# A cosine gate without Abs on ScalarE, and four pieces of work moved beside it

## The chip, the cores and the metric

The kernel runs on one core of one Trainium2 chip. The metric is the device time of one execution in microseconds (us), and a stated time is the median of several executions. PE is TensorE (matmuls), PEld its weight loads, ACT ScalarE, DVE VectorE, POOL GpSimd. "L467" is line 467 of the kernel whose profile is shown; the same line of the program has slightly other numbers in other kernels.

## The reference

Cross attention between tokens and 32 state rows per head makes a matrix of 4352 rows and 512 columns, which goes through a two-layer network whose gate is h times cos(h):

```python
scores = scale * x @ state.T          # softmax, then a @ state        (x reads)
scores2 = scale * state @ x.T         # softmax, then a2 @ x           (state reads)
x = concatenate([xread, sread])       # -> (4352, 512)
h = x @ w_in                          # (4352, 2048)
g = h * np.cos(h)
return g @ w_out                      # (4352, 512)
```

The two weight matrices arrive as 64-bit floats; ACT, DVE and POOL convert them on the way, in five pieces per block.

## The kernel before

The work is cut into 144 tiles ("steps"): per batch of 512 tokens 16 hidden tiles of 128 x 512, and 16 smaller ones for the states. One step, in the order of the program (cuts marked; the conversions run only in the first steps):

```python
def hidden(t):                        # PE: 2 matmuls into one of two PSUM buffers
    t.hp = hps.tile([P, S], F32, name="h")[:, 0:t.n]
    ...
def gate(t):                          # ACT: h + 1.5 * 2**23, to round h to an integer
    nc.scalar.activation(t.q, t.hp, func=ACTF.Copy, bias=MAGIC)
def gate2(t):                         # DVE: (q - MAGIC) - h
    nc.vector.scalar_tensor_tensor(out=t.q, in0=t.q, scalar=MAGIC, in1=t.hp,
                                   op0=ALU.subtract, op1=ALU.subtract)
def gate3(t):                         # ACT: |q|, then sin(pi/2 - 2 pi |q|) = cos(2 pi h)
    nc.scalar.activation(t.q, t.q, func=ACTF.Abs)
    nc.scalar.activation(t.q, t.q, func=ACTF.Sin, bias=halfpi, scale=-TWO_PI)
def gate4(t):                         # DVE: the product h * cos, into a slot of g_all
    nc.vector.tensor_tensor(t.g, t.hp, t.q, op=ALU.mult)
...
for step, t in enumerate(all_tiles):
    hidden(t)
    go(0)                             # attention work of PE
    gate(t); gate2(t)
    if step == 3:
        part(0, "products", 1, SIDE)
        part(0, "products_kept", 1, SIDE)      # two evictions on ACT
    go(1); go(3)                      # attention work of ACT, of DVE
    convert(last, "bcdf")             # DVE: shift, xor; POOL: sum; next load
    convert(conv, "1")                # ACT: first half of a conversion
    gate3(t); gate4(t)
    convert(conv, "2")                # ACT: second half
    go(2); go(4)                      # more attention work of ACT (exponentials), DVE
    ...                               # POOL: block sums; PE: outputs of earlier steps
```

(h is held divided by 2 pi.) After each batch's scores, ACT takes exponentials, which need another activation table than Sin: at these changes the trace has 15 table loads, 1.28 us each.

## Time and profile before

787.93 us, median of 3 executions (786.89 to 788.06); the profiled execution took 786.81 us with a span of 785.0 us at a granted clock of 1.00.

| engine | busy us | share of the span |
|---|---|---|
| PE | 765.1 | 97% |
| DVE | 417.3 | 53% |
| ACT | 389.1 | 50% |
| POOL | 176.7 | 23% |

The table alone says that PE is nearly full. What it can't say is which of PE's 20 idle microseconds wait for what: that is in the timeline, whose lines end with the idle time before a group and who ended it. The prediction shows those lines.

### The profile page before, as it was taken

How to read it: one execution, taken by the hardware profiler on the slowest of the kernel's cores; microseconds unless marked ns; L12 is line 12 of the kernel's file. 1: busy time of each engine (PE TensorE's matmuls, PEld its weight loads, DVE VectorE, ACT ScalarE, POOL GpSimd, SP SyncE). 2: the span in 40 equal slices, each digit the busy share in tenths (PEclk: the TensorE clock that was granted, in tenths of full speed). 3: DMA queues.
4: the chain of work that ended last, by engine and by line, in shares of the span. 5: the costliest groups of instructions: out<-in, count | busy, mean ns of one | idle time of the engine just before them, and what ended most of it. 6: DMA issues, size and time to landing. Idle time of an engine off the chain costs nothing.

```text
span 785.0 us, 7535 instructions
## 1 busy us (share of the span) xinstructions
PE 765.1 (97%) x2664; PEld 340.3 (43%) x2664; DVE 417.3 (53%) x656; ACT 389.1 (50%) x626; POOL 176.7 (23%) x118
## 2 busy tenths in 40 slices
PE   8998899899999999999999999999999999999997
PEld 3443433344344444444344434434444444455554
DVE  5768778623563466734554467635554446431431
ACT  3888954733463545633473446443563445322222
POOL 2344359673000000641000001640000004610200
PEclk9999999999999999999999999999999999999999
DMA  8595451060011510250104310330100114000021
GB/s 241 167 263 187 141 100 28 4 104 1 3 25 31 102 24 5 34 101 0 24 5 76 58 27 15 54 67 0 28 1 0 28 28 130 4 0 15 13 41 40
DMA packets 161957, 43.49 MB, mean 55 GB/s; under 512 B 153920, under 2 KB 153920, under 8 KB 161920
## 3 DMA queue, kind: packets, MB, share of 16 engines
q1 hardware_dynamic: 161024, 42.49, 24.8%
q10 hardware_dynamic: 768, 0.39, 0.2%
q8 instruction: 21, 0.34, 0.2%
q0 software_dynamic: 128, 0.13, 0.1%
q14 instruction: 16, 0.13, 0.1%
HBM read 34.08 MB, written 8.91 MB: 55 GB/s over the span
## 4 chain that ended last, share of the span: by engine, by line
PE 81%; ACT 10%; DVE 6%; issue 1%; DMA 1%; SPq 0%; POOL 0%; DVEq 0%
PE o L532 44%; PE h L467 26%; PE at L314 4%; PE o L652 4%; PE at L404 2%; ACT q L482 1%; ACT q L481 1%; ACT s L228 1%; DVE q L476 1%; ACT q L473 1%; DVE g_all L488 1%; ACT xT L360 1%; ACT w_in L225 1%; ACT L482 1%; DVE xT L334 1%
## 5 line engine op out<-in xcount | busy, mean ns | idle before, releaser
L467 PE MATMUL h<-aT,sw 128*128 128x512 f32 x512 | 241.5, 594 | 11.0 <-DVE g_all L488 8.1
L532 PE MATMUL o<-g_all,w_out 128*128 128x512 f32 x512 | 236.4, 598 | 1.2 <-POOL w_out L239 1.2
L494 POOL TENSOR_TENSOR g_all<-g_all 128x512 f32<-128x512 f32 x80 | 112.1, 1423 | 451.5 <-DVE g_all L488 447.9
L473 ACT ACTIVATE q<-h 128x512 f32<-128x512 f32 (+1 forms) x144 | 82.1, 570 | 262.3 <-PE h L467 262.2
L476 DVE SCALAR_TENSOR_TENSOR q<-q,h 128x512 f32<-128x512 f32 (+1 forms) x144 | 94.2, 654 | 216.9 <-ACT q L473 216.9
L532 PE MATMUL o<-g_all,s 128*128 128x512 f32 x384 | 177.3, 598 | 0.0
L488 DVE TENSOR_TENSOR g_all<-h,q 128x512 f32<-128x512 f32 (+1 forms) x144 | 94.8, 658 | 124.8 <-ACT q L482 118.6
L467 PEld LDWEIGHTS h<-aT,sw 128*128 128x128 f32 x512 | 96.4, 190 | 135.4 <-issue 110.7
L532 PEld LDWEIGHTS o<-g_all,w_out 128*128 128x128 f32 x512 | 94.0, 190 | 125.5 <-issue 118.4
L481 ACT ACTIVATE q<-q 128x512 f32<-128x512 f32 (+1 forms) x144 | 87.6, 608 | 93.5 <-DVE q L476 93.4
L532 PEld LDWEIGHTS o<-g_all,s 128*128 128x128 f32 x384 | 70.8, 190 | 91.7 <-issue 87.3
L482 ACT ACTIVATE q<-q,halfpi 128x512 f32<-128x512 f32 (+1 forms) x144 | 100.5, 698 | 4.5
L239 POOL TENSOR_TENSOR w_out<-w_out,s 128x1024 int32<-128x1024 int32 x10 | 23.9, 2390 | 77.1 <-DVE w_out L234 73.5
L494 DVE TENSOR_TENSOR g_all<-g_all 128x512 f32<-128x512 f32 x48 | 33.2, 692 | 1.6
L441 ACT COPY sw<-at 128x512 f32<-128x512 f32 x50 | 26.8, 589 | 9.0 <-PE at L314 9.0
L467 PE MATMUL h<-sT,w_in 128*128 128x256 f32 x128 | 30.2, 379 | 0.0
L652 PE MATMUL o<-w_out,g_all 128*128 128x512 f32 x64 | 29.6, 592 | 0.0
L467 PEld LDWEIGHTS h<-sT,w_in 128*128 128x128 f32 x128 | 24.3, 190 | 10.1 <-issue 6.7
L239 POOL TENSOR_TENSOR w_in<-w_in,s 128x1024 int32<-128x1024 int32 (+1 forms) x10 | 19.3, 1929 | 38.8 <-DVE w_in L234 36.5
L314 PE MATMUL at<-w_in,stT 64*32 64x512 f32 x400 | 27.2, 601 | 0.0
L538 DVE SCALAR_TENSOR_TENSOR held<-o,held 128x512 f32<-128x512 f32 x40 | 25.3, 675 | 2.9 <-PE o L532 2.9
L559 DVE STREAM_TRANSPOSE ot<-held 128x512 f32<-128x512 f32 x32 | 22.1, 692 | 0.0
(80 smaller groups left out, 427.7 us busy)
## 6 DMA issues: line engine op xcount, KB each, us to landing
out_dram<-ot SPq DMA_DIRECT2D x132, 64.0 KB, 2.0
g_all<-in_moe_w_out_dram SPq DMA_DIRECT2D x8, 1024.0 KB, 4.9
g_all<-in_moe_w_in_dram SPq DMA_DIRECT2D x6, 1024.0 KB, 5.2
xT<-in_x_dram SPq DMA_DIRECT2D x96, 64.0 KB, 2.3
x_b<-in_x_dram SPq DMA_DIRECT2D x24, 256.0 KB, 4.6
x_b<-in_x_dram SPq DMA_DIRECT2D x16, 128.0 KB, 4.0
g_all<-in_moe_w_in_dram SPq DMA_DIRECT2D x4, 512.0 KB, 6.0
x_b<-in_moe_w_out_dram SPq DMA_DIRECT2D x1, 1024.0 KB, 5.9
```

The costliest lines, as they stand in the source:

```text
L239: nc.gpsimd.tensor_tensor(bits, bits, e, op=ALU.add)
L314: nc.tensor.matmul(out=(to or at)[j][Ns * k:Ns * k + Ns, 0:n], lhsT=w[D * j:D * j + D, self.b, Ns * k:Ns * k + Ns], rhs=r(slice(D * j, D * ...
L441: (copy or nc.scalar.copy)(sw_of[self.b, nt][:, j, c0:c1], to[j][:, 0:c1 - c0])
L467: nc.tensor.matmul(out=t.hp, lhsT=t.lhs(i), rhs=t.rhs(i), start=(i == 0), stop=(i == t.kn - 1))
L473: nc.scalar.activation(t.q, t.hp, func=ACTF.Copy, bias=MAGIC)
L476: nc.vector.scalar_tensor_tensor(out=t.q, in0=t.q, scalar=MAGIC, in1=t.hp, op0=ALU.subtract, op1=ALU.subtract)
L481: nc.scalar.activation(t.q, t.q, func=ACTF.Abs)
L482: nc.scalar.activation(t.q, t.q, func=ACTF.Sin, bias=halfpi, scale=-TWO_PI)
L488: nc.vector.tensor_tensor(t.g, t.hp, t.q, op=ALU.mult)
L494: engine.tensor_tensor(out, a, b, op=ALU.subtract)
L532: nc.tensor.matmul(out=acc[bank][ch], lhsT=w[:, i, P * ch:P * ch + P], rhs=g.g, start=(i == 0), stop=(i == NH - 1))
L652: nc.tensor.matmul(out=acc[MAIN][i], lhsT=t.g[:, P * i:P * i + P], rhs=w_out[:, :, t.f, :], start=(t.n_th == 0), stop=(t.n_th == NF - 1))
```

## The change

The intent is to take work off ACT. The gate converts h + 1/4 to an integer n (ACT's output is an integer). Rounded to nearest, n − h lies between −1/4 and 3/4 and pi/2 − 2 pi (n − h) between −pi and pi; Sin is given that directly, without Abs. The rounding was not looked at by itself. Around it four pieces of work move: five weight conversions, two evictions (copies of results out of PSUM, the matmuls' output memory), batch 1's last product copies, and the block sums (sums and differences of blocks of w_out on POOL, which later products use as weights). Cut to its core:

```diff
-        nc.scalar.activation(t.q, t.hp, func=ACTF.Copy, bias=MAGIC)
+        nc.scalar.activation(t.q.bitcast(I32), t.hp, func=ACTF.Copy, bias=0.25)
-        nc.vector.scalar_tensor_tensor(out=t.q, in0=t.q, scalar=MAGIC, in1=t.hp, ...)
+        nc.vector.tensor_tensor(t.q, t.q.bitcast(I32), t.hp, op=ALU.subtract)
-        nc.scalar.activation(t.q, t.q, func=ACTF.Abs)
...
-            if b == 1 and nt > 0:               # batch 1's last product copies: DVE -> ACT
+            if b == 1 and 0 < nt < 3:
...
-        (0, 1, 2, 3, 4, 5, 6, 7, 8, 10, 11, 12, 13, 14))}   # steps of the conversions
+        (0, 1, 2, 3, 4, 5, 6, 7, 8, 11, 12, 13, 14, 15))}
...
-                22: (ALU.subtract, s3, a11, a21, lo),       # block sums on POOL; the
-                23: (ALU.subtract, s3, a11, a21, hi)}       # others go one step later
+                32: (ALU.subtract, s3, a11, a21, lo),
+                33: (ALU.subtract, s3, a11, a21, hi)}
...
                 part(0, "products", 1, SIDE)
-                part(0, "products_kept", 1, SIDE)
...
         gate3(t)
+        if step == 3:
+            part(0, "products_kept", 1, SIDE)
```

More of the change, by code (lines that the diff above doesn't have):

```diff
@@ L16 @@
 PSUM = bass.MemoryType.PSUM
-MAGIC = 12582912.0
 TWO_PI = 2.0 * math.pi
@@ L472, in gate @@
         t.q = msb.tile([P, S], F32, name="q")[:, 0:t.n]
-        nc.scalar.activation(t.q, t.hp, func=ACTF.Copy, bias=MAGIC)
+        nc.scalar.activation(t.q.bitcast(I32), t.hp, func=ACTF.Copy, bias=0.25)
     def gate2(t):
-        nc.vector.scalar_tensor_tensor(out=t.q, in0=t.q, scalar=MAGIC,
-                                       in1=t.hp, op0=ALU.subtract,
-                                       op1=ALU.subtract)
+        nc.vector.tensor_tensor(t.q, t.q.bitcast(I32), t.hp, op=ALU.subtract)
     def gate3(t):
-        nc.scalar.activation(t.q, t.q, func=ACTF.Abs)
         nc.scalar.activation(t.q, t.q, func=ACTF.Sin, bias=halfpi,
@@ L822 @@
     lo, hi = slice(0, NH // 2), slice(NH // 2, NH)
-    block_at = {15: (ALU.add, s1, a21, a22, lo),
-                17: (ALU.add, s1, a21, a22, hi),
-                18: (ALU.subtract, s2, s1, a11, lo),
-                19: (ALU.subtract, s2, s1, a11, hi),
-                20: (ALU.subtract, s4, a12, s2, lo),
-                21: (ALU.subtract, s4, a12, s2, hi),
-                22: (ALU.subtract, s3, a11, a21, lo),
-                23: (ALU.subtract, s3, a11, a21, hi)}
+    block_at = {16: (ALU.add, s1, a21, a22, lo),
+                18: (ALU.add, s1, a21, a22, hi),
+                19: (ALU.subtract, s2, s1, a11, lo),
+                20: (ALU.subtract, s2, s1, a11, hi),
+                21: (ALU.subtract, s4, a12, s2, lo),
+                22: (ALU.subtract, s4, a12, s2, hi),
+                32: (ALU.subtract, s3, a11, a21, lo),
+                33: (ALU.subtract, s3, a11, a21, hi)}
     LAG = 3
```

## The prediction

> **What bounds the kernel now.** I read the page first, then sums over windows, then the idle gaps of the TensorE timeline, then the queues of ScalarE and VectorE ahead of each gap. The chain that ended last and three windows (columns: stretch in us and its length, then busy us of PE, PEld, DVE, ACT, POOL, then clock, DMA share, GB/s):
>
> ```profile
> PE 81%; ACT 10%; DVE 6%; issue 1%; DMA 1%; SPq 0%; POOL 0%; DVEq 0%
> ```
>
> ```profile
> 0.00:22.00 22.00, 18.80 (x78) 8.47 (x79) 13.56 (x22) 8.38 (x14) 5.57 (x12) 1.00 0.86 240
> 22.00:155.00 133.00, 121.97 (x510) 52.16 (x510) 97.19 (x145) 102.77 (x153) 71.22 (x38) 1.00 0.45 127
> 155.00:785.00 630.00, 624.29 (x2078) 279.63 (x2076) 306.56 (x490) 277.99 (x462) 99.93 (x69) 1.00 0.19 34
> ```
>
> TensorE (PE) bounds it, at a full clock. After 155 us it is busy 624 of 630 us, though ScalarE (ACT) is busy only 278. Between 22 and 155 us, where weights are converted beside the first steps, ACT is busy 103 of 133 and PE has 11 us idle. Before 22 us no gate has run. So the question is which PE gaps lie behind the gate. The larger ones (start, length, group, in brackets the idle time before it and who ended it):
>
> ```profile
> 32.94 1.99 PE L467 MATMUL h<-aT,sw 128*128 128x512 f32 x4 [0.66 <-DVE g_all L488]
> ...
> 45.13 1.98 PE L532 MATMUL o<-g_all,w_out 128*128 128x512 f32 x4 [1.16 <-POOL w_out L239]
> ...
> 76.10 1.98 PE L467 MATMUL h<-aT,sw 128*128 128x512 f32 x4 [1.95 <-DVE g_all L488]
> ...
> 83.45 1.98 PE L467 MATMUL h<-aT,sw 128*128 128x512 f32 x4 [2.43 <-ACT sw L441]
> ...
> 102.99 1.98 PE L467 MATMUL h<-aT,sw 128*128 128x512 f32 x4 [1.21 <-DVE g_all L488]
> ```
>
> ```profile
> 146.14 1.98 PE L467 MATMUL h<-aT,sw 128*128 128x512 f32 x4 [1.86 <-DVE g_all L488]
> ...
> 151.69 1.98 PE L467 MATMUL h<-aT,sw 128*128 128x512 f32 x4 [0.97 <-DVE g_all L488]
> ```
>
> ```profile
> 322.76 1.98 PE L467 MATMUL h<-aT,sw 128*128 128x512 f32 x4 [0.71 <-DVE g_all L488]
> ```
>
> ```profile
> 493.83 1.98 PE L467 MATMUL h<-aT,sw 128*128 128x512 f32 x4 [0.70 <-DVE g_all L488]
> ```
>
> With 0.54 at 54.55 (ACT copy of tokens) and 0.26 at 59.87 (states kept), these eleven sum to 12.45 us. A gap also costs its pipeline restart: the matmuls before 76.10 start at 72.27 and go every 0.429 us, so the next was due at 73.99 and lost 2.11, not 1.95; some 0.16 more for each. Call it 14 us in all, 1.8% of 788: **the change can't win more than that by emptying ACT.** Most gaps end with VectorE's product h times cosine (L488), because the hidden tiles have two PSUM buffers and tile t+2 needs tile t's product.
>
> [...] The trace has 608 (Abs) and 698 (Sin, bias pointer)[...] and Copy to an integer should cost what Copy to a float does (570; the 128x1024 conversions take 1.15 us to integers and 1.16 to floats). [...] one shift takes 1.82 us instead of 0.69 while a GpSimd sum runs[...].
>
> **The change part by part.** PE's program is the same, instruction for instruction, in both kernels; only waits can shrink.
>
> (1) Abs goes:
>
> ```profile
> L481 ACT ACTIVATE q<-q 128x512 f32<-128x512 f32 (+1 forms) x144 | 87.6, 608 | 93.5 <-DVE q L476 93.4
> ```
>
> 87.6 us of ACT work, nearly all beside PE. Abs to Sin is 0.66 from start to start, since Sin waits for Abs's result. Copy with bias 0.25 and integer output replaces Copy with the magic bias; one tensor-tensor subtraction replaces the two-operation one, 0.69 against L488's 0.69: nothing. So each gate is 0.66 us shorter, and in steps 0 to 15 ACT's queue 16 × 0.66 = 10.6 us.
>
> (2) One effect is larger than 0.66. After each batch's exponentials the Sin table must be reloaded, and now the load stands behind Abs, which waits for DVE. Without Abs it stands right behind Copy and runs while DVE subtracts. Take ACT ahead of the gap at 83.45:
>
> ```profile
> 77.20 0.59 ACT L473 ACTIVATE q<-h 128x512 f32<-128x512 f32 x1
> 77.68 1.19 ACT L225 ACTIVATE w_out<-g_all 128x1024 f32<-128x1024 f32 x1
> 78.75 0.64 ACT L481 ACTIVATE q<-q 128x512 f32<-128x512 f32 x1
> 79.40 1.28 ACT L482 ACT_TABLE_LOAD   x1
> 80.70 0.72 ACT L482 ACTIVATE q<-q,halfpi 128x512 f32<-128x512 f32 x1
> 81.32 1.11 ACT L228 ACTIVATE s<-g_all 128x1024 int32<-128x1024 uint32 x1
> 82.33 0.58 ACT L473 ACTIVATE q<-h 128x512 f32<-128x512 f32 x1
> ```
>
> (3) The last five conversions come one step later, so step 10, shown here, loses its two conversion pieces. Now: the previous Sin ends 0.66 earlier, exps too, Copy at about 76.5, load 77.0 to 78.3, Sin to 78.95, next Copy 78.9, the eviction that PE wants 79.4 and 79.9. Its first half is done at 79.95; PE is ready for it at 81.0 (83.45 − 2.43). VectorE's product of that tile, after the row sums, ends near 80.3. The gap goes whole: 2.6 us. DVE gets a shift and an xor (1.9 us) more in step 16, whose product ended 3 us before it was needed: bearable.
>
> (4) Step 3's two evictions go behind Sin. Before, ACT idles 2.37 us for PE's products at 38.8 to 41.14 with a conversion, Abs and Sin of a finished tile behind it. Afterwards those fill the wait: Sin of step 3 at some 38 instead of 43.81. Its weight block lands at 37.5, close but in time. Two or three Abs less make the three steps before it 1.1 to 1.8 us earlier, by walking the queue. That takes the gaps at 32.94 (0.8) and 45.13 (1.3), and with ACT ahead those at 54.55 and 59.87 (0.8).
>
> (5) Batch 1's last product copies go from DVE (1.27 us at 147.74) to ACT, and the s3 block sums (2.4 us each on GpSimd at 135.9 and 140.3) leave for steps 32 and 33, where GpSimd is idle after 185 us. s3 is first used at step 35, two to three steps of 5 to 6 us later. At 146.14 I walk: Sin 0.66 earlier, exps end 140.7, load beside the subtraction, but DVE's row sums hold the product to about 144.6, where PE is ready at 144.3: gain 1.5 of 2.0. At 151.69 DVE loses the 1.27 copies: gap gone, 1.1.
>
> At 322.76 and 493.83 the chain of (2) saves about a microsecond: both gone, 0.85 each. At 102.99 the tile was ready at 95.35 but Copy ran at 97.84, behind a conversion; with ACT ahead it goes 2 us earlier: gone, 1.4.
>
> At 76.10 I expect **nothing**. DVE is in one unbroken run:
>
> ```profile
> 66.12 0.69 DVE L476 SCALAR_TENSOR_TENSOR q<-q,h 128x512 f32<-128x512 f32 x1 [0.47 <-ACT q L473]
> ...
> 71.51 0.68 DVE L476 SCALAR_TENSOR_TENSOR q<-q,h 128x512 f32<-128x512 f32 x1
> ...
> 75.36 0.68 DVE L488 TENSOR_TENSOR g_all<-h,q 128x512 f32<-128x512 f32 x1
> ```
>
> Its head waits for a Copy at 65.49, right as PE finished that tile. So nothing in the 9.9 us is ACT's, and the 2.1 lost there stay.
>
> Sum: 0.8 + 1.3 + 0.8 + 2.6 + 1.4 + 1.5 + 1.1 + 1.7 = 11.2 us. I take off 1.2, my guess for small new gaps, since everything now runs closer to transfers and to DVE. 787.93 − 10.0 = 777.9.
>
> **Rivals.** (a) ACT bounds: then 87.6 us gone would bring tens of microseconds. PE at 624 of 630 us after 155 speaks against it; time under 772 is nearly out of reach. (b) VectorE or the transfers take over in 20 to 105 us: as ACT runs ahead, DVE (16.25 of 20 us busy at 60 to 80) becomes the wait at more places than 76.10, and weight blocks landing 4.8 to 6.1 us after issue become late. For: the head of step 3 has half a microsecond to spare. Against: most blocks land 4 us before use. It would leave half the gain: 782 to 784. (c) The moves hurt: the step 3 eviction, now behind a conversion that waits on a transfer, delays tile 4, or late s3 and late conversions stall the second product: 785 to 792. Each has slack of at least about a microsecond in my walk, so I give it little. (d) The gap at 76.10 also closes: 775.5.
>
> **Range and chances.** 775.0 to 782.0: from (d) with no new gaps to a good part of (b). Faster by over 2% means under 772.2, more than all the gaps: 0.02. Slower by over 2% needs 15.8 us of new waits: 0.01.
>
> **What would show it.** ACT busy should fall by 87 to about 302 us, PE's idle from 20 to about 10. The gaps at 45, 83, 103, 151, 322 and 494 should be gone, that after 72 still near 2 us with the same DVE run ahead of it, that at 146 near 0.4. Sin's table load should start half a microsecond after Copy. I am wrong if PE waits on a weight transfer or on s3, if the gap at 76 goes, or if PE's step period after 155 us moves at all.

## The result

The changed kernel takes 775.92 us (median of 4 executions, 775.32 to 777.2); the kernel before took 787.68 us beside it. The ratio is 0.9854, with a 95% interval of 0.9838 to 0.9869. The output is correct.

The chain that ended last, of the changed kernel, and its crowded stage (same columns as in the prediction):

```profile
PE 93%; DVE 3%; ACT 1%; DMA 1%; POOL 0%; issue 0%; ACTq 0%; POOLq 0%
```

```profile
22.00:155.00 133.00, 130.27 (x546) 56.66 (x545) 99.59 (x152) 90.64 (x131) 76.50 (x43) 1.00 0.47 130
```

ACT had 10% of the chain and has 1%; PE is now busy 130.3 of these 133 us, not 122.0. Over the whole run ACT is busy 305.7 us (389.1 before), while PE's 763.0 us are nearly what they were (765.1).

The PE groups that answer to those in the prediction:

```profile
32.98 1.98 PE L465 MATMUL h<-aT,sw 128*128 128x512 f32 x4 [0.42 <-DVE g_all L484]
...
43.88 1.98 PE L528 MATMUL o<-g_all,w_out 128*128 128x512 f32 x4 [0.36 <-POOL w_out L237]
...
73.74 1.98 PE L465 MATMUL h<-aT,sw 128*128 128x512 f32 x4 [1.94 <-DVE g_all L484]
...
78.49 1.88 PE L465 MATMUL h<-aT,sw 128*128 128x512 f32 x4
...
96.74 1.98 PE L465 MATMUL h<-aT,sw 128*128 128x512 f32 x4
```

```profile
137.87 1.95 PE L465 MATMUL h<-aT,sw 128*128 128x512 f32 x4
...
142.25 1.89 PE L465 MATMUL h<-aT,sw 128*128 128x512 f32 x4
```

```profile
312.36 1.88 PE L465 MATMUL h<-aT,sw 128*128 128x512 f32 x4
```

A line without brackets had no idle time before it worth printing. Six of the nine gaps shown before are gone (the last, at 482.45 now, isn't shown); two are smaller, and that of tile 11 stands as it was.

PE's program is the same in both kernels, 2664 records in the same order. So I can subtract the start of each record in one trace from the start of the same record in the other, and see where the difference jumps. This gives the account of the whole gain, read to about 0.1 us in this pair of traces. It is not that exact from trace to trace: between runs whose edits lie elsewhere, start-up differs by up to 1.5 us and the products of step 7 by up to 0.5, so these two rows are not safely the change's.

| PE record (start before → after) | jump, us | idle before it, before → after |
|---|---|---|
| start-up, tokens' transfer (6.32 → 6.72) | +0.40 | 0.20 → 0.60 |
| tile 3 (32.94 → 32.98) | −0.37 | 0.66 → 0.42 |
| products of step 3 (near 40) | −0.43 | |
| first output (45.13 → 43.88) | −0.80 | 1.16 → 0.36 |
| token transposes (54.55 → 52.59) | −0.70 | 0.54 → 0 |
| products of step 7 (59.87 → 57.52) | −0.40 | 0.26 → 0 |
| tile 11 (76.10 → 73.74) | 0 | 1.95 → 1.94 |
| tile 12 (83.45 → 78.49) | −2.60 | 2.43 → 0 |
| tile 16 (102.99 → 96.74) | −1.30 | 1.21 → 0.02 |
| tile 26 (146.14 → 137.87) | −2.02 | 1.86 → 0 |
| tile 27 (151.69 → 142.25) | −1.17 | 0.97 → 0 |
| tiles at 322.76 and 493.83 | −0.97 each | 0.71, 0.70 → 0 |

They sum to −11.33; with smaller jumps the end is at −11.48, which is the difference of the spans (785.0 and 773.5).

ACT's queue ahead of tile 12, which the prediction walked, now reads (start, length, operation):

```profile
74.18 0.59 ACT L472 ACTIVATE q<-h 128x512 int32<-128x512 f32 x1
74.79 1.28 ACT L478 ACT_TABLE_LOAD   x1
76.09 0.72 ACT L478 ACTIVATE q<-q,halfpi 128x512 f32<-128x512 f32 x1
76.72 0.58 ACT L472 ACTIVATE q<-h 128x512 int32<-128x512 f32 x1
77.19 1.06 ACT L439 COPY sw<-at 128x512 f32<-128x512 f32 x2
```

The table load starts 0.61 us after Copy, where it took 2.20 us before (77.20 to 79.40). It runs beside DVE's subtraction (from 74.81), Sin starts 1.30 us after the load does (74.79 to 76.09), and the evictions start 3.0 us after Copy, not 5.6. DVE's run ahead of tile 11 is unbroken as it was:

```profile
63.77 0.69 DVE L475 TENSOR_TENSOR q<-q,h 128x512 f32<-128x512 int32 x1 [0.47 <-ACT q L472]
...
69.16 0.68 DVE L475 TENSOR_TENSOR q<-q,h 128x512 f32<-128x512 int32 x1
...
73.00 0.68 DVE L484 TENSOR_TENSOR g_all<-h,q 128x512 f32<-128x512 f32 x1
```

From 63.77 to 73.00 are 9.23 us; before, from 66.12 to 75.36, 9.24. The subtraction with an integer input takes 0.69 us, as the old one did.

### The profile page after: what moved, and what is told of

It reads as the page before. It is cut to its first block, busy times and chain, and to the rows that moved or that the text cites. A ratio compares the mean times of both kernels' runs of the same rounds, so it can differ in the third digit from the quotient of the medians.

```text
span 773.5 us, 7528 instructions
## 1 busy us (share of the span) xinstructions
PE 763.0 (99%) x2664; PEld 340.6 (44%) x2664; DVE 414.3 (54%) x654; ACT 305.7 (40%) x484; POOL 177.3 (23%) x118
## 4 chain that ended last, share of the span: by engine, by line
PE 93%; DVE 3%; ACT 1%; DMA 1%; POOL 0%; issue 0%; ACTq 0%; POOLq 0%
PE o L528 50%; PE h L465 31%; PE at L312 4%; PE o L648 4%; PE at L402 2%; PE o L312 1%; PE at L385 1%; DMA g_all<-in_moe_w_in_dram 1%; DMA s<-in_state_dram 0%; DVE i L326 0%; PE o L705 0%; DVE xT L332 0%; DVE w_out L232 0%; POOL w_out L237 0%; ACT s L226 0%
## 5 line engine op out<-in xcount | busy, mean ns | idle before, releaser
L475 DVE TENSOR_TENSOR q<-q,h 128x512 f32<-128x512 int32 (+1 forms) x144 | 94.3, 655 | 274.2 <-ACT q L472 274.1
L472 ACT ACTIVATE q<-h 128x512 int32<-128x512 f32 (+1 forms) x144 | 82.5, 573 | 345.4 <-PE h L465 345.2
L332 DVE STREAM_TRANSPOSE xT<-i 128x1024 f32<-128x1024 f32 x16 | 19.8, 1236 | 0.0
```

The costliest lines, as they stand in the source:

```text
L472: nc.scalar.activation(t.q.bitcast(I32), t.hp, func=ACTF.Copy, bias=0.25)
L475: nc.vector.tensor_tensor(t.q, t.q.bitcast(I32), t.hp, op=ALU.subtract)
```

## The experiments

All twelve runs gave a correct result. The kernel before ran beside each of them, at medians of 786.95 to 787.18 us. "Offset" is the jump of PE's record starts against the changed kernel, computed as above. The changed kernel was timed in a session of its own, and the interval of a ratio is about 0.3% wide, more than 2 us; so most of these runs can't be told from the changed kernel by their times. The offsets are sharper, and the readings rest on them, but each comes from one execution.

### The gate alone

The changed gate, in the old schedule:

```diff
 # the kernel before, with
+ bias=0.25, integer output; tensor_tensor subtract; no Abs
```

> The new gate (integer near h + 1/4, no Abs) in the old schedule; all four moves undone. My theory: the gate and the moves close different gaps. From the queues of the changed kernel: with the conversion pieces of step 10 back, ACT's eviction after the first exponentials comes about 2.1 us later and TensorE loses some 1.4 us at tile 12; with batch 1's copies back on VectorE the product at step 25 ends 1.3 us later and tile 27 loses some 1.2 us. Sum about 778.7 us, saving 9 of the 12. Rival (the gate does all of it, the moves are decoration): 776. Rival (the moves do most of it): 783 or more.

Measured: 777.92 us (777.78 to 779.11), ratio 0.9881 (0.9867 to 0.9896). Against the kernel before, its offsets have all the jumps of the table but that of tile 27 (0.97 us of idle time left). Against the changed kernel it loses 1.04 us at tile 27, as expected, and 1.5 us near 75 us, which was not what I had expected: tile 12 shows no gap, but PE was slow just before (a granted clock of 0.50 from 75 to 78 us), which can hide a gap of that size. So this trace doesn't show that the gate alone closes tile 12's gap; the run with the conversions back is the better test. More of the slow stretch below.

What follows: the gate brings 9.3 us by the medians of its rounds (787.18 − 777.92), the whole change 11.8 by those of its own (787.68 − 775.92). The moves are the smaller part on top of it.

### The moves alone

```diff
 # the changed kernel, with
+ bias=MAGIC; scalar_tensor_tensor; Abs, then Sin
```

> The four moves with the old gate (magic bias, Abs). My theory: tile 12's gap shrinks from 2.4 to about 0.2 us (step 10 has no conversion pieces), tile 27's goes (1.1), ACT's token copy in time (0.5), but the gaps at tile 16, tile 26, and the two later batches (322 and 494 us before) stay: about 783.5 us. If the gate does all, 787 to 788. If the moves do most, under 780.

Measured: 786.63 us, median of 6 executions from 784.61 to 787.7; ratio 0.9986 (0.9974 to 0.9999). The trace is that of the 784.61 us execution (span 782.8) and is what I expected but for two places: tile 12 keeps 1.21 us of idle time, not 0.2, and tile 16's gap grows from 1.21 to 2.14 us, as I read it because the conversions now crowd that step while Abs is still there. Tile 27's gap is gone, tile 26's and the later two (0.70 and 0.71) are not. So the moves without the gate are worth 2.2 us in the best execution and 0.6 us in the median. The other five executions are 1.3 to 3.1 us slower than the profiled one; their mean clocks (0.993 to 0.998) may account for a part, but one at 787.28 had 0.998. That spread stays open.

What follows: the moves can't be what made the time, but they do more once the queue is lighter: at tile 16 the moves do harm while Abs is there (0.93 us more), and none without it. That it is the conversions' shift among the four was not tested.

### The table load held up

```diff
+        if step in (10, 24, 40, 56, 72, 88, 104):
+            nc.scalar.activation(t.q[:, 0:1], t.q[:, 0:1], func=ACTF.Copy)
         gate3(t)
```

> The changed kernel with one more ACT operation of one column (a copy of q onto itself) between VectorE's subtraction and Sin in the seven steps that follow a batch's exponentials, so that the Sin table load waits for VectorE again, as it did behind Abs. The operation itself is about 0.2 us. My theory (the load beside the subtraction is a part of the gain of its own): Sin ends 0.8 to 0.9 us later in these steps; VectorE's row sums hide about half of it; TensorE loses 0.1 to 0.5 us in some of the seven: 776.5 to 777.5 us, gaps of up to 0.5 us back before tile 26 and its fellows. Rival (only Abs's 0.66 us and the lighter queue matter): 775.9, no new gap.

ACT in step 10 of this run:

```profile
75.28 0.20 ACT L874 ACTIVATE q<-q 128x1 f32<-128x1 f32 x1 [0.75 <-DVE q L475]
75.50 1.28 ACT L478 ACT_TABLE_LOAD   x1
```

Measured: 776.57 us (775.75 to 777.52), ratio 0.9861 (0.9848 to 0.9874). The load starts 1.57 us after Copy (73.93), not 0.61. The offsets are +0.29 at tile 12, +0.31 at tile 16 and +0.58 at tile 26 (0.42 us of idle time), and nothing in the later batches. The sum, 1.2 us, lies where I expected it, but the medians differ by 0.65 us with overlapping ranges. So it is seen in the trace and unsafe in the times.

What follows: the load that runs beside the subtraction is a real part of the gain at tile 26, at most some half a microsecond of its 2.0: of the 0.96 us by which the load is later, 0.22 are the added operation itself. The rest there is Abs itself, in the step before and in the step.

### Conversions back

```diff
-        (0, 1, 2, 3, 4, 5, 6, 7, 8, 11, 12, 13, 14, 15))}
+        (0, 1, 2, 3, 4, 5, 6, 7, 8, 10, 11, 12, 13, 14))}
```

> The changed kernel with the last five weight conversions where they were (steps 10 to 14); all else new. My theory: in step 10 the first conversion piece stands again between Copy and the table load and the second between Sin and the next Copy, some 2.2 us on ACT; the eviction that tile 12 needs is half done 1.3 to 1.4 us after TensorE could take it: a gap of that size before tile 12, 777.2 us. With the gate alone the same queue cost nothing visible, but there TensorE ran at half clock just before, so it was hidden. Rival (the shift has no use once Abs is gone): 775.9 and no gap at tile 12.

ACT in step 10, and PE at tile 12:

```profile
75.06 1.16 ACT L223 ACTIVATE w_out<-g_all 128x1024 f32<-128x1024 f32 x1
...
78.16 1.13 ACT L226 ACTIVATE s<-g_all 128x1024 int32<-128x1024 uint32 x1
```

```profile
80.29 1.98 PE L465 MATMUL h<-aT,sw 128*128 128x512 f32 x4 [1.24 <-ACT sw L439]
```

Measured: 776.49 us (775.83 to 777.19), ratio 0.986 (0.9843 to 0.9876). The gap is there as expected: 1.24 us of idle time, an offset of +1.41. The median shows only 0.57 of it. Part of the reason may be the clock: three of the changed kernel's four executions have a mean clock of 0.997 or 0.998, three of this run's four have 1.0 (see the runs with the sums back and the gap filled).

### Copies back

```diff
-            if b == 1 and 0 < nt < 3:
+            if b == 1 and nt > 0:
```

> The changed kernel with batch 1's last product copies on VectorE again (1.27 us in step 25). My theory, from the run with the gate alone: a gap of 0.9 to 1.0 us before tile 27, nothing else: 776.9 us. Rival (ACT, now lighter, makes up for it): 775.9.

```profile
142.69 1.98 PE L465 MATMUL h<-aT,sw 128*128 128x512 f32 x4 [0.97 <-DVE g_all L484]
```

Measured: 776.72 us (775.87 to 778.05), ratio 0.9866 (0.9851 to 0.9881); one new offset, +1.20 at tile 27, which the line shows. As expected: ACT does not make up for it, since the product at step 25 stands behind the copies on DVE.

### Step 3's evictions back

```diff
                 part(0, "products", 1, SIDE)
+                part(0, "products_kept", 1, SIDE)
...
         gate3(t)
-        if step == 3:
-            part(0, "products_kept", 1, SIDE)
```

> The changed kernel with step 3's evictions ahead of the conversion and Sin again. I credited this move, with the missing Abs, with part of the 2.1 us gained before 46 us. From the run with the gate alone, where TensorE was as early there as in the changed kernel, I now expect that it earns nothing on TensorE: ACT idles 3.2 us instead of 1.3 ahead of the evictions, step 4's Copy comes about 1.1 us later, and no TensorE gap follows: 775.9 us, within 0.3. If my first account holds: 776.6 or more, with a larger gap before the product at 43.9 us.

Measured: 775.53 us (774.98 to 776.88), ratio 0.9852 (0.9837 to 0.9867). ACT idles 3.21 us ahead of the evictions instead of 1.32, the first output waits 0.37 us instead of 0.36, and no offset beyond start-up is as large as 0.15 us. My account in the prediction falls: this move earns nothing that the trace shows. Nor did it with Abs there: in the trace of the moves alone, tile 3 waits 0.66 us and the first output 1.12, as before.

### Sums back

```diff
-                32: (ALU.subtract, s3, a11, a21, lo),
-                33: (ALU.subtract, s3, a11, a21, hi)}
+                23: (ALU.subtract, s3, a11, a21, lo),
+                24: (ALU.subtract, s3, a11, a21, hi)}
```

> The changed kernel with the s3 block sums in pair one (steps 23 and 24) instead of steps 32 and 33, one step later than in the kernel before. My theory: GpSimd's place for them costs TensorE nothing[...]: 775.9 us, no new gap above 0.3 us between 125 and 160 us. Rival (the sums were what lengthened VectorE's run there): a gap of 0.5 to 2 us before tile 26 or 27, 776.5 to 778.

Measured: 776.35 us (774.55, and three at 776.33 to 776.37), ratio 0.9856 (0.9839 to 0.9872). No gap or offset between 125 and 160 us. What differs is near 75 us, and no block sum is near it: sums over four microseconds there (columns as in the prediction; the one after the busy times is the clock), first of this run, then of the changed kernel:

```profile
74.00:78.00 4.00, 4.00 (x21) 0.61 (x19) 3.42 (x7) 2.97 (x4) 1.28 (x1) 0.57 0.76 258
```

```profile
74.00:78.00 4.00, 4.00 (x23) 1.27 (x23) 3.12 (x7) 3.97 (x8) 1.59 (x1) 1.00 0.77 262
```

PE was granted a clock of 0.5 from 74.56 for 3.41 us and so 0.57 in the mean of these four; PE looks equally busy in both, which is how such a stretch hides. It costs an offset of 1.3 us. The execution of this run with a mean clock of 1.0 took 774.55 us, those with 0.997 and 0.998 took 776.35. So the sums' place is worth nothing that I can see.

### Abs back from step 16 on

```diff
+        if step >= 16:
+            nc.scalar.activation(t.q, t.q, func=ACTF.Abs)
         gate3(t)
```

> The changed kernel with Abs put back from step 16 on (it does not change the result: cosine is even), so that 128 of 144 gates have it, and all of the weight-conversion stage has not. My theory: nearly all of ACT's saving (77 of 87 us) is in this part and is hidden, and only the steps behind a batch's exponentials pay: gaps of 1.9, 0.7 and 0.7 us before tile 26 and in batches 4 and 6, each with 0.16 to 0.25 us of restart, as in the run with the moves alone: 779.5 to 780 us. Rival (the gain was all in the crowded stage before step 16): 775.9.

```profile
141.08 1.98 PE L465 MATMUL h<-aT,sw 128*128 128x512 f32 x4 [1.86 <-DVE g_all L484]
```

Measured: 779.67 us (778.69 to 780.51), ratio 0.9905 (0.989 to 0.992). The offsets are +1.92 at tile 26, +0.92 and +0.97 in the two later batches, 3.8 us in all; the medians differ by 3.75. (Its trace also has the half-clock stretch, another 1.3.) As expected. Of 128 Abs, three places are all that one pays for.

### The product first in step 9

```diff
-            elif last >= 0:
+            elif last >= 0 and step != 9:
                 convert(last, "bcdf")
...
         gate4(t)
+        if step == 9:
+            convert(last, "bcdf")
```

> The changed kernel with one line moved: in step 9 VectorE does the product h times cosine before the shift and xor of a weight conversion (0.69 + 1.23 us), not after. My theory of the one large gap that stayed (1.94 us before tile 11, VectorE unbroken for 9.9 us): the gap goes to at most 0.2, the conversion is 0.6 us later and not missed: 773.9 us. Rival (what follows the gap, the exponentials and the table loads on ACT, sets the pace anyway): the idle time moves to tile 12 and the time stays at 775.5 to 776.

```profile
78.73 1.95 PE L465 MATMUL h<-aT,sw 128*128 128x512 f32 x4 [0.68 <-DVE g_all L484]
```

Measured: 775.45 us (774.78 to 776.88), ratio 0.9849 (0.9836 to 0.9861). Tile 11's idle time went from 1.94 to 0.08 us, an offset of −1.86; then +0.84 came at tile 12 (the line) and +0.45 at tile 16. PE's products of step 11, too, take 1.64 us instead of 1.09: all but two of them start at 75.06 or later, when ACT's last exponential, which reads the PSUM banks that they write, has ended. My theory holds for the gap and falls for the gain; the rival was mostly right. (This trace is also 1.2 us later than the changed kernel's by 12 us, 1.0 of it in a half-clock stretch that starts at 8.49 us; more of that below.) The exponentials, which stand behind DVE's subtraction and Sin in step 9, set the pace next.

### More out of the run

```diff
-            if step == 1: convert(4, "bcdf")
-            elif last >= 0: convert(last, "bcdf")
+            if last >= 0 and step not in (1, 3, 8, 9): convert(last, "bcdf")
...                                  # step 3's now stands ahead of go(3)
         gate4(t)
+        if step == 1: convert(4, "bcdf")
+        if step == 9: convert(11, "bcdf"); convert(12, "bcdf")
```

> The changed kernel with four conversions on VectorE placed later or earlier: step 1's and steps 8's and 9's shifts and xors behind the product of steps 1, 9 and 9, step 3's ahead of the state reads. Moving step 9's alone moved the idle time from tile 11 to tile 12, because the exponentials on ACT, which wait for the shift and the subtraction in VectorE's run, set the pace next. Taking step 8's conversion out of the run too lets Sin and the exponentials of step 9 start 1.8 us earlier. If VectorE's run is the whole cause of what stayed at tiles 11 to 12, the 2.1 us there go, and 0.5 each at 33 and 44 us: 772.6 to 773.5 us, clear of both kernels. If another wait takes their place (the weight block of step 11 late on GpSimd is the likeliest), 774.5 to 776.

DVE and POOL in step 9 of this run:

```profile
73.37 3.25 DVE L232 SCALAR_TENSOR_TENSOR w_out<-g_all,w_out 128x1024 int32<-128x1024 int32 x1
```

```profile
72.88 2.66 POOL L237 TENSOR_TENSOR w_in<-w_in,s 128x1024 int32<-128x1024 int32 x1 [6.76 <-DVE w_in L232]
```

Measured: 777.42 us (777.2 to 778.65), ratio 0.9877 (0.9862 to 0.9891): slower than the changed kernel. Tiles 3 and 11 gained 0.50 and 2.22 as meant. But step 1's later conversion made the products of step 3 wait 0.59 us for POOL, and the xor of step 9, which takes 1.23 us elsewhere, ran beside POOL's sum and took 3.25, so that tile 12 waited 1.69 us. It was the rival that I had called likeliest, late work on POOL, with its partner on DVE, but the time lies above the range of either forecast.

### The shift later too

From the run with the product first, step 8's conversion stays in place; instead batch 1's shift, which ACT doesn't wait for as early, goes behind step 9's subtraction:

```diff
-            y_dve[s[3]].append((b, "shift"))
+            if b == 1:
+                x_dve[s[4]].append((b, "shift"))
+            else:
+                y_dve[s[3]].append((b, "shift"))
...                                  # step 3's conversion ahead of go(3), step 9's after gate4
```

> The run that put step 9's conversion behind the product, with two more moves: batch 1's shift from the end of step 8 to step 9, behind that step's subtraction, so that Sin and the exponentials start 1.2 us earlier while step 8's conversion stays where GpSimd needs it; and step 3's conversion ahead of the state reads on VectorE. In the last attempt a shift and xor taken out of step 8 came back as an xor of 3.25 us beside a GpSimd sum. My theory: tile 11's gap stays gone, tile 12's shrinks from 0.68 to 0.3 us or less, the one at 44 us goes (0.5): 773.5 to 774.5 us, 1.5 to 2 us under the changed kernel. If the exponentials are not what tile 12 waits for: 775 to 775.5.

```profile
76.95 1.96 PE L465 MATMUL h<-aT,sw 128*128 128x512 f32 x4 [0.53 <-DVE g_all L484]
...
95.66 1.98 PE L465 MATMUL h<-aT,sw 128*128 128x512 f32 x4 [0.39 <-DVE g_all L484]
```

Measured: 774.05 us (773.74 to 774.24), ratio 0.9834 (0.9819 to 0.9848), so better than both kernels, by 1.9 us in the medians against the changed one. Tile 12 still waits 0.53 us, more than expected, tile 16 0.39, and the 0.5 us at 44 us did not come: the first output waits 0.24 us instead of 0.36. The offset from 10 us to the end is about −1.3, but 0.45 of that lies at the products of step 7, where other runs whose edits lie elsewhere differ as much; some 0.8 is left for the moves. The intervals of the two ratios overlap. Its four executions are also much closer together than the changed kernel's. The last experiment is about why.

### The gap filled

```diff
+        if step == 11:
+            warm(2, acc[SIDE][0])        # two matmuls on leftover data, result unused
         hidden(t)
```

> The changed kernel with two matmuls on leftover data (1.72 us of TensorE time, result unused) ahead of tile 11, in the 1.94 us in which TensorE idles for VectorE. Three traces (the gate alone, the sums back, Abs from step 16 on) show TensorE at a granted clock of 0.5 for 3.41 us that begins about a microsecond after this idle time, and 1.3 to 1.6 us lost there; six others with the same idle time don't. If the idle time is what calls for the half clock: no half-clock stretch near 75 us, no execution of the run below 0.998 in mean clock but for the start, and 774.5 to 775.3 us, as the changed kernel's undisturbed executions, although TensorE has more to do. If the half clock comes of itself: executions on both sides again, and some at 776.3.

```profile
70.90 1.88 PE L705 MATMUL o<-g_all 128*128 128x512 f32 x4
73.02 1.98 PE L465 MATMUL h<-aT,sw 128*128 128x512 f32 x4 [0.24 <-DVE g_all L484]
```

Measured: 774.88 us (774.56 to 775.42, five executions), ratio 0.9848 (0.9835 to 0.9862). PE has 1.7 us more to do, and nothing after it is later: tile 11 starts at 73.02 (73.74 in the changed kernel), and the 0.7 us between them lie at start-up (0.3) and at the products of step 7 (0.4). All five executions have a mean clock of 0.999 or 1.0; of the changed kernel's four, three have 0.997 or 0.998. By the trace of the gate alone the stretch starts at 74.67, 0.8 us after tile 11 starts, and lasts 3.41 us.

That is less than it seems. The trace of the run with the product first, in which tile 11's idle time is gone, has a half-clock stretch too, at start-up (columns as in the prediction; the clock is the 0.50):

```profile
8.49:11.90 3.41, 3.39 (x26) 2.25 (x25) 1.72 (x3) 1.82 (x3) 0.00 (x0) 0.50 1.05 384
```

So a mean clock of 0.997 doesn't say where it was lost, and of unprofiled executions I have no more than that. For the idle time speaks that 22 of 38 executions with it are below 0.999 (all kernels with the moves or the new gate), and 2 of 17 without it. Against it: of the ten traces with this idle time, seven have no such stretch, and in the kernel before 2.43 us of idle time at tile 12 aren't followed by one either; and the kernel before, with the same idle time, was at 1.0 in five of nine executions beside this run but in three of 25 beside the others, so sessions differ. That the idle time at tile 11 is what lets the clock fall is likely, not shown. Nor is a gain in time: the median is 1.0 us below the changed kernel's, but the intervals of the two ratios overlap and the trace has its lead from before tile 11.

## Why the prediction was right

The time was predicted at 777.9 us within 775.0 to 782.0, and is 775.92. The time alone would suit rival (d), the gap at 76.10 closing as well (775.5), better than 777.9; the trace decides against (d), since that gap stands at 1.94 us. By its own steps:

**The bound.** PE's idle time was the whole account: 14 us to win at most, 11.5 won, and PE's record starts show no jump anywhere but at the listed gaps. After 155 us nothing moved but the two places named.

**(1) Abs.** ACT lost 83.4 us of busy time (389.1 − 305.7) and not 87: Abs's 87.6 overlapped its neighbours by some 3 us, two copies of 0.59 us came back, and the new Copy and Sin are some 3 ns slower in the mean (573 and 701 ns, from 570 and 698). (These means, like the 608 and 698 of the prediction, mix tiles of 512 and of 256 columns. For 512 alone the trace before has 632 ns for Abs and 722 for Sin.) Of all this PE sees 0.9 to 2.0 us at each of a few places. Shown by the run with Abs back from step 16 on.

**(2) The table load.** Shown in the trace, and by holding it up: at most 1.2 us of offsets in all. I had given it credit at 322 and 494 us as well; there the held load cost nothing, so those two gaps are Abs's alone.

**(3) The conversions.** Right, and shown: without this move 1.41 us of the 2.60 at tile 12 would be lost again.

**(4) Step 3's evictions.** This step failed in its cause. The gains that I gave to it and the missing Abs together, 0.8 at tile 3 and 1.3 at the first output, came out as 0.37, and 0.43 + 0.80, half a microsecond less; 0.42 and 0.36 us of idle time are left, where I had both gaps gone. And putting the evictions back loses none of it. ACT had time to spare there; the first output waits for DVE's and POOL's conversion, whose start, by the trace, hangs on the Copy of step 3 (its subtraction starts at 37.54, the xor at 40.09, POOL's sum at 41.46). The gate alone shows the same jumps.

**(5) Batch 2.** The copies are worth 1.20 us at tile 27, shown (predicted 1.1). At tile 26 I left about 0.4 us of gap, and all of it closed (2.02, predicted 1.5): DVE's product ended 3.69 us after Copy started (134.09 to 137.78), I had walked about 3.9 (140.7 to 144.6), and PE took tile 26 at 137.87. The block sums' place, which I listed with this, shows no effect.

**The rest.** Tile 16: 1.30 (predicted 1.4). Later batches: 0.97 each (0.85). The tokens and the products of step 7: 1.1 (0.8). Tile 11: nothing, with the same DVE run, as predicted.

**The sum.** 11.2 us were predicted term by term and 11.5 came. That the sums agree so well is in part luck: the first 46 us brought 0.5 less than their terms, the tokens, tile 26 and the later batches some 1.0 more, and start-up took 0.4 back. I then took off 1.2 us for new small gaps, and that is the term that was mis-sized: the traces show none that costs PE. Transfers did become late for ACT, by 0.75 and 0.37 us (at 50.49 and 96.08), but PE never waited for it. Of the rivals, (b) did not come true in the changed kernel; it did when I tried to close tile 11's gap as well, where an xor on DVE and a sum on POOL ran beside each other and took 3.25 and 2.66 us (1.23 and about 2.36 elsewhere).

What I had not seen at all is the clock. In three traces a half-clock stretch follows PE's idle 1.94 us at tile 11 and costs another 1.3 to 1.6 us. If the idle time is its cause, which isn't shown, a gap's price is not only its length.

## What to carry to other kernels

When one engine is full, list its idle gaps first: they are the most that any relief of another engine can bring (here an estimated 14 us, of which 11.5 came), and each gap is walked back on its own. A gap closes only as far as the next chain allows, so ask what would arrive second (at tile 11, 1.86 us won gave back 0.84 and 0.45 at tiles 12 and 16); and at a table switch, let the load stand where it needn't wait for another engine (held up by 0.96 us here, it cost up to 0.58 us at one tile). Align two traces by the records of the engine whose program didn't change: where the difference jumps is where the time went, even where the medians scatter by more. Compare several such traces before believing a jump of half a microsecond.
